# When the weights of pass 3's second half and of pass 4 are fetched, and where B11 is split, in a linear-attention kernel with two MLPs on one Trainium2 core

## The chip, the cores and the metric

One core of a Trainium2 chip runs the whole program. The metric is device microseconds (us) of one execution. TensorE is written PE (PEld for its weight loads), VectorE DVE, ScalarE ACT, GpSimd POOL; SP is the engine whose queue issues nearly all transfers. "Granted clock" is the share of TensorE's full clock that it was given; TensorE has two levels, 2.4 GHz (1.00) and 1.2 GHz (0.50).

## The reference

```python
kv  = einsum('bhsd,bhse->bhde', k, v)          # 8 batches, 8 heads, 576 positions, head 64
out = einsum('bhsd,bhde->bhse', q, kv)
x   = out / sqrt(mean(out*out, -1) + 1e-6) * g_norm      # -> 4608 tokens x 512
h   = x @ w_in1;  x = maximum(0.01*h, h) @ w_out1        # 512 -> 2048 -> 512
h   = maximum(x @ w_in2, 0);  return (h*h) @ w_out2      # 512 -> 2048 -> 512
```

## The kernel before

The 4608 tokens are 9 blocks of 512 (`TB`). Four passes follow each other on TensorE:

- pass 1: attention and the first product (`gemm1`), and on the side the preparation of all weights, which go to DRAM as `w2_d`;
- pass 2 (`second(0, ...)`): the first MLP's second product;
- pass 3 (`first`): the second MLP's first product, then the squared ReLU (`square`), whose result goes to DRAM as `g_d[1]`;
- pass 4 (`second(1, ...)`): the second MLP's second product, to the output.

Every float32 operand is split into a rounded high part (ACT, line 554, suffix h) and a remainder (DVE, line 559, suffix l), and a product is three matmuls: high by high, high by low, low by high. Passes 2 to 4 use a scheme of seven block products for a 2x2 block matrix product (`PRODUCTS`, in the order 6, 1, 2, 7, 5, 4, 3). Its operands are quarters (for tokens of pass 3: B11, B21, B22) and sums of quarters (T1 to T4, made on DVE at line 539). The seven operands of one set of tokens in pass 3 come in the order T2, B11, B21, T3, T1, T4, B22. The results are put together by copies and additions that read the PSUM banks: ACT copies product 1 (`p`, line 605), DVE adds (line 574), and the four finished blocks C11, C22, C21, C12 of `h_C` are squared (ACT 621, 623, 624; DVE 626).

A **slot** is one call of `first` (6 matmuls of 512 columns, or 12 of 256) or `second` (12 matmuls of 256 columns). Each of passes 2 to 4 has 252 slots. Pass 3 begins at slot `t2` and pass 4 at `t3`; at the seam the last calls of `first` alternate with the first calls of `second`. Pass 3 runs over `SETS` (block 0 alone, then pairs of blocks): first all sets with the first half of the weights (14 of 28 tiles), then, from the last set on, with the second half. `again` is true for the one set that stands at that turn. In pass 4, blocks are taken in groups of seven slots; each group's `g_raw` (two loads of 512 KB, `load_g2`, line 512) is read back from DRAM.

The order of all this is written out: every step is an event with a slot number (`at_slot`), the events are sorted, and each engine's instructions stand in that order. An engine, and SP's queue, goes through its own list strictly in order; a waiting instruction holds what stands behind it. What the change touches:

- `fetch` (lines 275 to 281): takes the next tile of weights from the list `wanted` as long as fewer than `w_cap` are held and one of 45 buffers is free (`take_big` hands out the buffer that was returned longest ago), and issues its load of 512 KB (line 280). `cap` and `want` set the bound and the list; `drop_w` returns tiles.
- `tick` (lines 231 to 237), called at each slot: issues the stores that `store` put on a list two slots earlier (line 236). In pass 3 these are the `h_C` blocks, 256 KB each, four for every seven slots. `h_C` has four buffers (`hp`, line 97), so a block can't be written before the store of the one four earlier has landed.
- `prep` (lines 771 to 779): the order in which one set's operands are made: `os` sums, `oh` high parts, `ol` low parts. Lines 815 to 824 give each step its slot, 0.7 slots apart.

```python
at_slot(t0 + 1.5, "cap", 24)                       # 846, at the turn of pass 3
at_slot(t0 + 1.6, "want", (1, 0), NSLOT // 2, NSLOT)
at_slot(t3 - 26, "cap", 20)                        # 849, for pass 4
at_slot(t3 - 25.9, "want", (1, 1), 0, NSLOT)
at_slot(t3 + 6, "cap", 28)
```

Of the kernel before, what the change touches and what calls it, by code (L numbers as in the profile page):

```python
# [18 lines left out]
def tile_linear_attention_two_mlps(  # L19
# [108 lines left out]
    def take_big(shape, dtype, name):  # L128
        n = big_free.pop(0)
        return big.tile(shape, dtype, tag=f"s{n}", name=name), n  # L130

    def give_big(*ns):
        big_free.extend(ns)
# [95 lines left out]
        stores.append([out, in_, slots, 0])  # L229

    def tick():
        for x in stores:
            x[3] += 1
        while stores and stores[0][3] > 1:
            to, src, slots, _ = stores.pop(0)
            nc.sync.dma_start(out=to, in_=src)  # L236
            give_big(*slots)

    def sum_w2(w, n, name):
        a, b, op = SUMS[name]  # L240
        if (w, n) not in w_s:
            w_s[w, n] = take_big([P, 4, 2, P], F32, f"ws_{w[0]}{w[1]}_{n}")
        t = w_s[w, n][0][:, int(name[1]) - 1]
        nc.vector.tensor_tensor(out=t, in0=w_operand(w, n, a), in1=w_operand(w, n, b), op=op)
        w_s[w, n, name] = t
# [15 lines left out]
            give_big(w_s.pop((w, n))[1])  # L261


    wanted = []
    w_cap = [0]

    def want(w, a, b):
        wanted.extend((w, n) for n in range(a, b))
        fetch()

    def cap(n):
        w_cap[0] = n
        fetch()

    def fetch():
        while wanted and w_used[0] < w_cap[0] and big_free:
            w, slot = wanted.pop(0)
            t, n = take_big([P, 2, TB], F32R, f"w2_{w[0]}{w[1]}_{slot}")
            w_used[0] += 1
            nc.sync.dma_start(out=f32(t), in_=w2_d[w][slot])  # L280
            w_t[w, slot] = t, n

    def drop_w(*keys):
        for key in keys:
            give_big(w_t.pop(key)[1])
            w_used[0] -= 1
        fetch()
# [190 lines left out]
    def leaky(j, m):  # L478
        h = hp.tile([P, TB], F32, tag="h", name=f"h{j}_{m}")
        nc.scalar.activation(out=h, in_=h_ps.pop((j, m)), func=AF.Prelu, alpha=0.01)  # L480
        store(
            g_d[0][j][m // 4][:, m % 2, :, (m // 2 % 2) * U:(m // 2 % 2 + 1) * U],
            h.rearrange("p (t u) -> p t u", t=2),
        )
        tick()
# [95 lines left out]

    def first(u, z, pairs, x, free):
        tick()
        pr = ORDER[x]
        bk = "b" if pr in (6, 7, 4) else "a"
# [55 lines left out]
    def second(ph, gg, x, free):  # L641
        j, n = gg
        tick()
        pr = ORDER[x]
        if n == 0:
# [61 lines left out]
    with tc.manual_schedule():  # L707
# [44 lines left out]
        for s, (j, m) in enumerate(slots):  # L752
            if m == 0 and j + 1 < NB:
                at0, pace = (s - 4, 4) if j else (s, 4)
# [13 lines left out]
        def at_slot(t, *st):  # L768
            ev.append((t, st))

        def prep(z):
            n = (("os", 1), ("os", 2), ("oh", 2), ("oh", 11), ("ol", 2), ("oh", 0), ("ol", 11),
                 ("os", 3), ("ol", 0), ("oh", 3), ("oh", 1), ("ol", 3), ("ol", 1), ("os", 4))
            if z == "S":
                n += (("oh", 22), ("oh", 4), ("ol", 22), ("ol", 4))
            else:
                n += (("oh", 4), ("oh", 22), ("ol", 4), ("ol", 22))
            names = {11: "A11", 0: "A12", 22: "A22"} if z == "S" else {11: "B11", 0: "B21", 22: "B22"}
            return [(kind, names.get(x) or f"{z}{x}") for kind, x in n]

        def second_pass(t0, ph, blocks):
            gs = [(j, n) for j in blocks for n in range(NQ)]
            steps = prep("TS"[ph])
            for x, gg in enumerate(gs):
                at0 = t0 + NPR * x
                at_slot(max(at0 - 14, t0 - 12), "gl", ph, gg)
                for n, (kind, name) in enumerate(steps):
                    at_slot(at0 - 8 + n * NPR / len(steps) + 0.3, kind, ph, gg, name)
                at_slot(at0 - 8 + NPR + 0.31, "rawd", ph, gg)
                for n in range(NPR):  # L790
                    at_slot(at0 + n + 0.1, "s2", ph, gg, n, True)
                if gg[0] == blocks[-1]:
                    at_slot(at0 + NPR, "wd", (ph, 1), gg[1])
            return t0 + NPR * len(gs)
# [11 lines left out]
        for x, (half, z) in enumerate(insts):  # L806
            t0 = t2 + NPR * u
            pairs = [(n,) for n in range(half * NPAIR // 2, (half + 1) * NPAIR // 2)]
            if len(SETS[z]) == 1:
                pairs = [pairs[0] + pairs[1], pairs[2] + pairs[3]]  # L810
            again = x + 1 < len(insts) and insts[x + 1][1] == z
            if not (x and insts[x - 1][1] == z):
                lead = 11 if x and len(SETS[insts[x - 1][1]]) == 1 else 15
                at_slot(t0 - lead - XLEAD if x else t0 - 19, "xl", z)
                for y, (kind, name) in enumerate(prep("T")):
                    at0 = t0 - lead + 0.7 * y
                    if kind in ("oh", "ol"):
                        nth = [PRODUCTS[p][1] for p in ORDER].index(name)
                        if nth >= EARLY:
                            at0 = max(at0, t0 - 6.6 + 2 * (nth - EARLY) + (0.8 if kind == "ol" else 0))  # L820
                    elif name == "T4":
                        at0 = t0 - lead + 0.7 * y
                        at0 = max(at0, t0 - 6.6 + 2 * (4 - EARLY) + 0.9)
                    at_slot(at0, kind, 2, z, name)
                    if kind == "ol" and name == "T3":
                        at_slot(at0 + 0.01, "sd", z, "T3")
                    if kind == "ol" and name == "T1":
                        at_slot(at0 + 0.01, "sd", z, "T1")
                    if kind == "ol" and name == "T4":
                        at_slot(at0 + 0.01, "sd", z, "T4")  # L830
                        at_slot(at0 + 0.02, "sd", z, "T2")
                    if kind == "ol" and name == "B22":
                        at_slot(at0 + 0.01, "rawd", 2, z)
            for y, mine in enumerate(pairs):
                free = y == len(pairs) - 1 and not again
                for n in range(NPR):
                    at0 = t2 + NPR * u + 2 * n
                    at_slot(at0, "f", u, z, mine, n, free)
                    c = {2: "C11", 5: "C22", 4: "C21", 3: "C12"}.get(ORDER[n])
                    if c:  # L840
                        at_slot(at0 + 1.2, "sq", u, z, mine, c)
                if again or x == len(insts) - 1:
                    at_slot(t2 + NPR * u + 12.4, "wd3", mine)
                u += 1
            if again:
                at_slot(t0 + 1.5, "cap", 24)
                at_slot(t0 + 1.6, "want", (1, 0), NSLOT // 2, NSLOT)
        t3 = t2 + NPR * u
        at_slot(t3 - 26, "cap", 20)
        at_slot(t3 - 25.9, "want", (1, 1), 0, NSLOT)  # L850
        at_slot(t3 + 6, "cap", 28)
        second_pass(t3, 1, [j for half, z in insts if half for j in SETS[z]])
        ev.sort(key=lambda e: e[0])

# [26 lines left out]
        def drop_pairs(ps):  # L881
# [11 lines left out]
            "scale": scale_w, "join": join_w, "w": split_w, "g1": gemm1, "lk": leaky,  # L893
            "ws": sum_w2, "w2": split_w2, "want": want, "cap": cap, "xl": load_x, "gl": load_g2,
            "rawd": drop_raw, "os": sum_op, "sd": drop_sum, "oh": hi_op, "ol": lo_op,
            "tick": tick, "f": first, "sq": square, "s2": second, "wd": drop_group, "wd3": drop_pairs,
        }
        load = {
            "kv": (load_kv, 0, 2), "scale": (load_w, 0, 1), "a": (load_q, 1, 1)
# [21 lines left out]
        for kind, *args in prog:  # L921
            do[kind](*args)
            if kind in free_by:
                _, n, tiles = load[free_by[kind]]
# [34 lines left out]
```

## Time and profile before

| | us |
|---|---|
| median of 3 runs (lowest, highest) | 1663.08 (1662.37, 1665.74) |
| the profiled execution, its own time | 1666.68 |
| its span, first to last instruction | 1664.9 |
| PE busy in it | 1593.8 (96%) |
| DVE, ACT, POOL busy | 1218.7, 768.1, 255.1 |

In the trace, pass 2 begins at about 562 us, pass 3 at about 928, pass 4 at about 1286. A row of a timeline is: start, length, engine, line, operation, written tile, read tiles, shape, count; in brackets the idle time of that engine before it and what ended it. PE shows a matmul's length with its pipeline, so matmuls overlap; the step from one start to the next is what one costs. A row of windows gives the busy time of each engine in a stretch with the number of instructions, then the granted clock, the mean busy share of the 16 DMA engines, and what they moved in GB/s.

### The profile page before, as it was taken

To read this page: it belongs to the slowest core of one execution; us is meant where nothing else is said; L and a number is where in the kernel's file an instruction comes from. 1 tells how busy PE (TensorE), PEld (TensorE's weight loads), DVE (VectorE), ACT (ScalarE), POOL (GpSimd) and SP (SyncE) were. 2 spreads that over 40 slices of the span, in tenths; PEclk is the share of its full clock that TensorE was granted. 3 is DMA by queue.
4 is the path that set the end of the run, shared out by engine and by line. 5 is a ranking of instruction groups with operands and counts; after the bars stand their busy time and mean duration, and the time that the engine had idled before them with its cause. 6 is when DMAs were issued, how large, how long until landed. Compare 5 with 4: busy or idle time off the path is not lost. (4 is left out here: it accounts for less than half of the span.)

```text
span 1664.9 us, 27914 instructions
## 1 busy us (share of the span) xinstructions
PE 1593.8 (96%) x10504; PEld 1429.5 (86%) x10504; DVE 1218.7 (73%) x1867; ACT 768.1 (46%) x1439; POOL 255.1 (15%) x272
## 2 busy tenths in 40 slices
PE   4999999999999999999999999999999899999999
PEld 2778777777777899999999988778878899999999
DVE  5967777776675388878788877647776688888886
ACT  4555565655654344444434444424444344433433
POOL 3444544544554000000000000000000000000000
PEclk8999999999999999999999999999999999999999
DMA  7677988989977943333346654564449833333342
GB/s 215 197 210 242 329 283 276 318 268 303 349 248 269 410 155 127 127 128 129 135 136 227 211 173 162 193 212 152 158 158 326 312 127 128 131 130 127 133 133 83
DMA packets 249447, 338.45 MB, mean 203 GB/s; under 512 B 55264, under 2 KB 180192, under 8 KB 249312
## 3 DMA queue, kind: packets, MB, share of 16 engines
q1 hardware_dynamic: 249152, 336.67, 60.7%
q8 instruction: 83, 1.36, 0.3%
q14 instruction: 52, 0.43, 0.1%
q10 hardware_dynamic: 160, 0.00, 0.0%
HBM read 198.18 MB, written 138.41 MB: 202 GB/s over the span
## 5 line engine op out<-in xcount | busy, mean ns | idle before, releaser
L468 PE MATMUL hps<-xh,w 128*128 128x512 f32 x1152 | 374.0, 396 | 8.5 <-DVE sqo L413 6.2
L468 PEld LDWEIGHTS hps<-xh,w 128*128 128x128 f32 x1152 | 217.4, 189 | 57.1 <-DVE sqo L413 6.7
L468 PE MATMUL hps<-xl,w 128*128 128x512 f32 x576 | 226.0, 392 | 1.3 <-POOL xl L428 1.3
L468 PEld LDWEIGHTS hps<-xl,w 128*128 128x128 f32 x576 | 109.0, 189 | 23.1 <-POOL xl L428 2.1
L574 DVE TENSOR_TENSOR h_C<-aps,u 128x512 f32<-128x512 f32 x72 | 49.5, 688 | 70.4 <-DMA g<-h_C 37.4
L480 ACT ACTIVATE h<-hps 128x512 f32<-128x512 f32 x144 | 85.0, 592 | 34.0 <-DMA g<-h 30.8
L173 DVE TENSOR_SCALAR w_raw<-w_raw 128x512 uint32<-128x512 uint32 x64 | 48.6, 760 | 33.4 <-ACT wt L172 33.3
L574 DVE TENSOR_TENSOR u<-bps,p 128x512 f32<-128x512 f32 x72 | 49.5, 687 | 25.1 <-PE bps L595 13.7
L413 DVE SCALAR_TENSOR_TENSOR sqo<-ssps,sqo 128x512 f32<-128x512 f32 x36 | 24.9, 691 | 56.8 <-ACT sqo L412 55.9
L393 POOL TENSOR_TENSOR sqs<-sqo,sqs 128x512 fp32r<-128x512 f32 x36 | 49.2, 1367 | 85.5 <-DVE sqs L392 79.7
L190 DVE SCALAR_TENSOR_TENSOR wt<-wt,w_raw 128x512 uint32<-128x512 uint32 x64 | 58.0, 907 | 2.2
L595 PE MATMUL aps<-op_B22h,w 128*128 128x512 f32 (+1 forms) x160 | 53.4, 383 | 4.9 <-DVE h_C L574 4.9
L428 POOL TENSOR_TENSOR xl<-sqo,xh 128x512 fp32r<-128x512 f32 x36 | 48.4, 1344 | 60.8 <-ACT xh L427 43.4
L595 PE MATMUL aps<-op_B21h,w 128*128 128x512 f32 (+1 forms) x160 | 52.2, 375 | 4.9 <-ACT p L605 4.9
L612 ACT ACTIVATE h_C<-aps 128x512 f32<-128x512 f32 x36 | 21.6, 600 | 72.7 <-issue 29.9
L176 DVE SCALAR_TENSOR_TENSOR w_raw<-w_raw 128x512 uint32<-128x512 uint32 x64 | 52.9, 827 | 2.2
L605 ACT ACTIVATE p<-aps 128x512 f32<-128x512 f32 x36 | 21.3, 591 | 71.6 <-PE aps L595 71.6
L595 PE MATMUL bps<-op_T4h,w 128*128 128x512 f32 (+1 forms) x160 | 51.4, 370 | 1.2 <-DVE u L574 1.2
L595 PE MATMUL bps<-op_T3h,w 128*128 128x512 f32 (+1 forms) x160 | 52.0, 374 | 0.0
L595 PE MATMUL bps<-op_T2h,w 128*128 128x512 f32 (+1 forms) x160 | 51.3, 370 | 0.0
L595 PE MATMUL aps<-op_T1h,w 128*128 128x512 f32 (+1 forms) x160 | 51.0, 368 | 0.0
L595 PE MATMUL aps<-op_B11h,w 128*128 128x512 f32 (+1 forms) x160 | 51.0, 368 | 0.0
(1408 smaller groups left out, 4204.1 us busy)
## 6 DMA issues: line engine op xcount, KB each, us to landing
g_raw<-g SPq DMA_DIRECT2D x144, 512.0 KB, 5.6
w<-w SPq DMA_DIRECT2D x84, 512.0 KB, 7.3
g<-h SPq DMA_DIRECT2D x144, 256.0 KB, 5.7
g<-h_C SPq DMA_DIRECT2D x144, 256.0 KB, 2.4
w_raw<-in_moe_w_in_dram SPq DMA_DIRECT2D x32, 512.0 KB, 6.1
w_raw<-in_moe_w_out_dram SPq DMA_DIRECT2D x32, 512.0 KB, 5.9
w<-whS SPq DMA_DIRECT2D x64, 256.0 KB, 5.5
x_raw<-x SPq DMA_DIRECT2D x32, 512.0 KB, 6.1
```

What stands on the lines that cost most here:

```text
L173: nc.vector.tensor_scalar(out=upper, in0=upper, scalar1=0x80000000, scalar2=None, op0=ALU.bitwise_and)
L176: nc.vector.scalar_tensor_tensor(out=lower, in0=lower, scalar=29, in1=upper, op0=ALU.logical_shift_right, op1=ALU.bitwise_or,)
L190: nc.vector.scalar_tensor_tensor(out=t, in0=t, scalar=3, in1=lower, op0=ALU.logical_shift_left, op1=ALU.bitwise_or,)
L393: nc.gpsimd.tensor_tensor(out=sqs[:, 1], in0=sqo[:, 0], in1=f32(sqs[:, 0]), op=ALU.subtract)
L413: nc.vector.scalar_tensor_tensor(out=z, in0=ps, scalar=EPS, in1=z, op0=ALU.add, op1=ALU.mult)
L428: nc.gpsimd.tensor_tensor(out=xl, in0=osb, in1=f32(xh), op=ALU.subtract)
L468: nc.tensor.matmul(out=ps, lhsT=w[:, wh, c * P:(c + 1) * P], rhs=x_t[j][xh, c // 2][0][:, c % 2, :], start=(c == 0 and y == 0), stop=(c == ...
L480: nc.scalar.activation(out=h, in_=h_ps.pop((j, m)), func=AF.Prelu, alpha=0.01)
L574: nc.vector.tensor_tensor(out=t, in0=x, in1=y, op=ALU.add)
L595: nc.tensor.matmul(out=ps[:, p], lhsT=w[:, wh, c, :], rhs=t[xh][:, c, :], start=(fresh and p == 0 and c == 0 and y == 0), stop=(p == len(p ...
L605: nc.scalar.activation(out=p1, in_=ps, func=AF.Copy)
L612: nc.scalar.activation(out=h, in_=ps, func=AF.Relu)
```

## The change

Loads of weights can now be paced. `w_pace` is zero at first (no pacing). From the turn of pass 3 on it is 2: after a fetch, the next one is allowed two slots later; `tick` calls `fetch` at each slot. Just after pass 4's begin it becomes 1. The bounds change with it: 22 in place of 20 at `t3 - 26`, 24 at `t3 - 3`, and 28 at `t3 + 1` in place of `t3 + 6`. And in pass 3 the high part of B11 is made first of all steps of a set (it stood behind the two sums T1 and T2 and T2's high part); the three steps that it passes move back by one place (0.7 slots).

```diff
     def tick():
+        slot_n[0] += 1
...
             give_big(*slots)
+        if w_pace[0]:
+            fetch()
...
+    w_pace = [0]
+    w_next = [0]
+    slot_n = [0]
+
+    def set_pace(n):
+        w_pace[0] = n
...
         while wanted and w_used[0] < w_cap[0] and big_free:
+            if slot_n[0] < w_next[0]:
+                break
+            w_next[0] = slot_n[0] + w_pace[0]
             w, slot = wanted.pop(0)
...
-                for y, (kind, name) in enumerate(prep("T")):
+                todo = prep("T")
+                todo.insert(0, todo.pop(3))
+                for y, (kind, name) in enumerate(todo):
...
             if again:
+                at_slot(t0 + 1.4, "pace", 2)
                 at_slot(t0 + 1.5, "cap", 24)
...
-        at_slot(t3 - 26, "cap", 20)
+        at_slot(t3 - 26, "cap", 22)
         at_slot(t3 - 25.9, "want", (1, 1), 0, NSLOT)
-        at_slot(t3 + 6, "cap", 28)
+        at_slot(t3 - 3, "cap", 24)
+        at_slot(t3 + 1, "cap", 28)
+        at_slot(t3 + 1.1, "pace", 1)
```

No instruction is added or taken away on any engine; PE's and POOL's orders are the same. What moves is shown at three places.

**SP's queue at the turn of pass 3** (w_10_15 is the second of the 14 tiles of the second half; g<-h_C is a store of line 236). Before:

```order
L280 DMA w_10_15_11662<-w_10_15_148 128x1024
L280 DMA w_10_16_11664<-w_10_16_149 128x1024
L280 DMA w_10_17_11666<-w_10_17_150 128x1024
L280 DMA w_10_18_11668<-w_10_18_151 128x1024
L280 DMA w_10_19_11670<-w_10_19_152 128x1024
L280 DMA w_10_20_11672<-w_10_20_153 128x1024
L280 DMA w_10_21_11674<-w_10_21_154 128x1024
L280 DMA w_10_22_11676<-w_10_22_155 128x1024
L236 DMA g_6_1_250<-h_C_11655 128x2x256
L236 DMA g_5_1_246<-h_C_11697 128x2x256
```

After:

```order
L293 DMA w_10_15_11675<-w_10_15_148 128x1024
L237 DMA g_6_1_250<-h_C_11655 128x2x256
L293 DMA w_10_16_11696<-w_10_16_149 128x1024
L237 DMA g_5_1_246<-h_C_11683 128x2x256
L237 DMA g_7_0_253<-h_C_11692 128x2x256
L293 DMA w_10_17_11718<-w_10_17_150 128x1024
L237 DMA g_6_1_250<-h_C_11704 128x2x256
L293 DMA w_10_18_11737<-w_10_18_151 128x1024
```

Nine loads stood together ahead of the first store (w_10_14 with these eight); now two stand ahead of it, and one or two stores follow each load.

**SP's queue ahead of pass 4** (w_11_0 is the first tile of pass 4's weights). Before:

```order
L280 DMA w_11_0_13179<-w_11_0_161 128x1024
L280 DMA w_11_1_13181<-w_11_1_162 128x1024
L280 DMA w_11_2_13183<-w_11_2_163 128x1024
L280 DMA w_11_3_13185<-w_11_3_164 128x1024
L280 DMA w_11_4_13187<-w_11_4_165 128x1024
L280 DMA w_11_5_13189<-w_11_5_166 128x1024
L236 DMA g_4_3_244<-h_C_13163 128x2x256
```

After:

```order
L293 DMA w_11_0_13179<-w_11_0_161 128x1024
L237 DMA g_4_3_244<-h_C_13163 128x2x256
L293 DMA w_11_1_13192<-w_11_1_162 128x1024
L237 DMA g_3_3_240<-h_C_13189 128x2x256
L293 DMA w_11_2_13214<-w_11_2_163 128x1024
L237 DMA g_1_2_231<-h_C_13200 128x2x256
L237 DMA g_4_3_244<-h_C_13210 128x2x256
L293 DMA w_11_3_13234<-w_11_3_164 128x1024
```

Six loads stood ahead of a store; now one does. The same goes on up to w_11_27; the loads of group (7, 3)'s `g_raw` now stand behind 22 of pass 4's tiles, where they stood behind all 28.

**ACT in pass 3, at the set of blocks 3 and 4.** Before:

```order
L621 ACTIVATE h_C_10816<-h_C_10816 128x512
L554 ACTIVATE op_2_T2h<-sT_2_2_10841 128x1024
L554 ACTIVATE op_2_B11h<-x_raw_00_10727 128x1024
L605 ACTIVATE p_4_10875<-aps_1_10868 128x512
L612 ACTIVATE h_C_10898<-aps_1_10868 128x512
```

After:

```order
L634 ACTIVATE h_C_10816<-h_C_10816 128x512
L567 ACTIVATE op_2_B11h<-x_raw_00_10727 128x1024
L567 ACTIVATE op_2_T2h<-sT_2_2_10852 128x1024
L618 ACTIVATE p_4_10875<-aps_1_10868 128x512
L625 ACTIVATE h_C_10898<-aps_1_10868 128x512
```

The copy `p` now stands directly behind T2's high part. On DVE, one squaring (line 626) of the running set now stands ahead of the first sum of the next set, where it stood between its two sums.

## Rows read from the trace of the kernel before

**Rows 1.** Timeline of PE at the turn of pass 3, and later, ahead of pass 4.

```profile
1079.62 0.39 PE L595 MATMUL aps<-op_B21h,w 128*128 128x512 f32 x1
1084.41 0.80 PE L595 MATMUL aps<-op_B22h,w 128*128 128x512 f32 x1 [4.40 <-DVE h_C L574]
...
1264.24 0.50 PE L595 MATMUL aps<-op_B22h,w 128*128 128x512 f32 x1 [0.48 <-DVE h_C L574]
```

**Rows 2.** Windows: the wait at the turn, the stretch behind it, ahead of pass 4, behind its first wait.

```profile
1075.00:1084.40 9.40, 5.01 (x23) 3.81 (x21) 0.73 (x2) 0.60 (x1) 0.00 (x0) 0.95 1.01 384
1084.40:1091.00 6.60, 6.59 (x17) 5.22 (x18) 3.51 (x6) 2.37 (x4) 0.00 (x0) 0.55 0.57 183
...
1270.00:1292.00 22.00, 21.98 (x113) 18.53 (x113) 14.62 (x23) 9.49 (x17) 0.00 (x0) 1.00 1.04 390
...
1299.70:1306.60 6.90, 6.87 (x31) 6.32 (x32) 3.10 (x6) 2.35 (x4) 0.00 (x0) 0.59 0.70 230
```

**Rows 3.** Timeline of SP's queue at the turn of pass 3.

```profile
1067.84 4.91 SPq L280 DMA_DIRECT2D w<-w  x9
1073.75 12.19 SPq L236 DMA_DIRECT2D g<-h_C  x5
```

**Rows 4.** Stores of line 236 issued in 930 to 1065, 1073 to 1080, 1254 to 1262, 1270 to 1292, in turn.

```profile
DMA to landing us min/median/max: 2.1/2.3/7.8
...
DMA to landing us min/median/max: 7.8/8.8/9.8
...
DMA to landing us min/median/max: 6.9/7.1/8.4
...
DMA to landing us min/median/max: 5.7/8.1/8.8
```

**Rows 5.** Timeline of DVE ahead of pass 4, and of PE there.

```profile
1278.57 0.69 DVE L539 TENSOR_TENSOR sS_(7, 0)_13385<-g_raw,g_raw 128x512 f32<-128x512 f32 x1 [0.47 <-DMA g_raw<-g]
...
1285.86 0.69 DVE L574 TENSOR_TENSOR h_C<-bps,p 128x512 f32<-128x512 f32 x1 [0.87 <-DMA g<-h_C]
...
1290.21 0.69 DVE L574 TENSOR_TENSOR h_C<-aps,u 128x512 f32<-128x512 f32 x1 [1.86 <-DMA g<-h_C]
...
1298.95 0.68 DVE L574 TENSOR_TENSOR h_C<-bps,p 128x512 f32<-128x512 f32 x1
...
1299.73 2.90 PE L659 MATMUL ps<-w,op_(7, 0)_S 128*128 128x256 f32 x12 [3.90 <-ACT op_(7, 1)_S L554]
```

**Rows 6.** Timeline of ACT, then of PE, at the second set of pass 3.

```profile
968.77 1.06 ACT L554 ACTIVATE op_T2h<-sT 128x1024 fp32r<-128x1024 f32 x1 [3.96 <-DVE sT L539]
969.73 1.04 ACT L554 ACTIVATE op_B11h<-x_raw 128x1024 fp32r<-128x1024 f32 x1
970.68 0.58 ACT L605 ACTIVATE p<-aps 128x512 f32<-128x512 f32 x1
...
969.96 0.39 PE L595 MATMUL bps<-op_T4l,w 128*128 128x512 f32 x1
970.18 0.39 PE L595 MATMUL bps<-op_T4h,w 128*128 128x512 f32 x1
971.31 0.50 PE L595 MATMUL aps<-op_B21h,w 128*128 128x512 f32 x1 [0.74 <-ACT p L605]
```

**Rows 7.** Waits of PE in 960 to 1060, then in 1180 to 1240: in total, times, longest.

```profile
PE aps L595 <- ACT p L605: 2.2, 3, 0.7
...
PE aps L595 <- ACT p L605: 1.5, 2, 0.7
```

**Rows 8.** Windows around two short waits of PE in pass 1.

```profile
241.00:248.00 7.00, 5.46 (x35) 3.91 (x34) 4.51 (x6) 4.44 (x11) 4.38 (x6) 0.76 1.03 382
...
279.00:283.00 4.00, 1.71 (x11) 1.28 (x10) 3.63 (x7) 3.79 (x11) 2.97 (x4) 1.00 0.80 229
```

**Rows 9.** Line 280 in 1060 to 1330; then a line of the waits of SP's queue.

```profile
DMA to landing us min/median/max: 3.7/7.5/10.5
...
SPq L280 <- PE ps L659: 14.4, 12, 5.4
```

More of the change, by code (lines that the diff above doesn't have):

```diff
@@ L778, in prep @@
             names = {11: "A11", 0: "A12", 22: "A22"} if z == "S" else {11: "B11", 0: "B21", 22: "B22"}
+            assert n[3] == ("oh", 11)
             return [(kind, names.get(x) or f"{z}{x}") for kind, x in n]
@@ L895, in tile_linear_attention_two_mlps @@
             "rawd": drop_raw, "os": sum_op, "sd": drop_sum, "oh": hi_op, "ol": lo_op,
-            "tick": tick, "f": first, "sq": square, "s2": second, "wd": drop_group, "wd3": drop_pairs,
+            "tick": tick, "pace": set_pace, "f": first, "sq": square, "s2": second, "wd": drop_group, "wd3": drop_pairs,
         }
```

## The prediction

> **What bounds the kernel now.** I read the page first: TensorE is busy 96% of the span, so a change pays only where PE stands still or runs at its lower clock. Then the timeline of PE through pass 3 and into pass 4, looking for steps from one matmul start to the next that are longer than the usual 0.22 us [rows 6]; then, for each such place, the timelines of the engine that ended the wait. Three kinds of place turn up where the change works.
>
> *The turn of pass 3.* PE starts a matmul at 1079.62 and the next at 1084.41 [rows 1]: 4.79 us for a step of 0.22, a loss of 4.57. Behind it the granted clock is 0.55 for 6.6 us [rows 2], mostly the lower level, which costs another 0.45 x 6.6 = 2.97. The cause is in SP's queue: nine weight loads go out at 1067.84, and the stores of `h_C` come behind them [rows 3]. Nine loads of 512 KB are 4.72 MB, about 12 us at the 384 GB/s of that stretch [rows 2]. Those stores land after 7.8 to 9.8 us, against a median of 2.3 in the quiet part of pass 3 [rows 4]. There are four `h_C` buffers, so DVE can't write the next block, and PE waits for DVE.
>
> *The seam to pass 4.* PE idles 3.90 us before 1299.73 [rows 5], and the clock is 0.59 for the next 6.9 us, a loss of 0.41 x 6.9 = 2.83 [rows 2]. The row names ACT, but the addition on DVE at 1298.95 ends at 1299.63, 0.1 before PE starts: it empties a PSUM bank that this product takes over. DVE was late because it had itself waited 0.47 for `g_raw` and 0.87 and 1.86 for stores of `h_C` [rows 5], in a stretch in which transfers ran at 390 GB/s without a break [rows 2] and stores took a median of 8.1 us [rows 4].
>
> *The start of each set.* At 971.31 PE starts 1.13 us after the matmul before, 0.91 too late, behind `p` on ACT [rows 6]. ACT made T2's high part (968.77), then B11's (969.73), and only then `p` (970.68). The same wait, 0.7 us of idle, stands three times in 960 to 1060 and twice in 1180 to 1240 [rows 7]: five times 0.9.
>
> **The change, part by part.**
>
> *B11 ahead.* ACT idles 3.96 us before T2's high part, waiting for DVE's sum [rows 6]. B11's high part (1.04 us) needs no sum, only `x_raw`, so it goes into that idle time and costs nothing as long as the idle time is over 1.04 and `x_raw` is there: its loads are issued 10 slots (over 13 us) ahead of the step, while the slowest load of a weight, as large, takes 10.5 [rows 9]. `p` moves from 970.68 to 969.73, directly behind T2, and ends at 970.31; PE wants it at 970.18 + 0.22 = 970.40. So the whole 0.9 goes, five times: **4.5 us**. Bounds: nothing, if PE is then held by something else at once; 4.5 at most. I take 4.5, since rows 6 name no other wait. The squaring that changes places with a sum on DVE is as long a job in the same stretch; the second sum ends when it did. Cost nothing, covered by the same idle time of ACT.
>
> *Pacing at the turn.* The 14 loads are spread over 28 slots. Two slots (12 matmuls of 512 columns at 0.22 to 0.23: 2.7 us) now carry one load of 0.524 MB and on average 8/7 stores of 0.262, together 0.82 MB or 303 GB/s, under the 390 shown [rows 2]. A store then has at most one load ahead, 0.524 / 0.39 = 1.3 us, and lands after 2.3 + 1.3 = 3.6. Where stores took 6.9 to 8.4 us, at 1254 to 1262 [rows 4], PE idled 0.48 at 1264 [rows 1]; so 3.6 holds nobody. The wait and its lower clock go: 4.57 + 2.97 = 7.5. Bounds: 4.6, if the clock falls all the same, and 7.5. I take **7.2**, leaving 0.3 for small leftovers.
>
> *Pacing ahead of pass 4.* For the first 14 of the 26 slots, seven loads and ten stores are 6.3 MB in 19 us, 330 GB/s: no queue builds up. The last twelve slots carry six weights, six loads of `g_raw` and six stores, 7.86 MB in about 16.5 us, 476 GB/s, over the 390 shown. At 390 this takes 20.2 us, so 3.7 us of backlog are left at the end, and a store there lands after up to 2.3 + 3.7 = 6.0. That is under the 6.9 to 8.4 that cost 0.48. DVE's three waits go, 0.47 + 0.87 + 1.86 = 3.20, and the addition that PE waits for comes 3.2 earlier; PE keeps 0.7 of idle time there, since DVE's own work is then the limit. Does the clock still fall? In pass 1, one idle time of about 1.5 us (7.00 less 5.46 busy) goes with a fall to the lower level, another of 2.3 (4.00 less 1.71) doesn't [rows 8]. So I take a coin's toss over a fall half as long as the one here (1.4 us), 0.7. The gain is 3.2 + 2.83 - 0.7 = **5.3**. Bounds: 0, if DVE is held as before, and 3.9 + 2.83 = 6.7.
>
> A rule of the Trainium skill speaks against this term. Its page "DMA: Bandwidth & Descriptors", section "Where 436 GB/s comes from", has the HBM side bind transfers between HBM and SBUF at about 358 GB/s per core. By that figure the twelve slots would leave 5.5 us of backlog, a store would land after 7.8, and part of DVE's waits would stay. The trace shows 390 over 22 us, so the measurement decides here.
>
> *Are the weights in time?* The tile with the least room is fetched 12 slots before its use (w_11_17, 18, 24 and 25), over 16 us; loads of line 280 land within 10.5 us at the worst [rows 9], with the queue full. Cost nothing; without that room, PE would wait for the difference. Reads of `g_raw` move ahead of some weights and come earlier, which pays nothing on PE.
>
> Sum: 4.5 + 7.2 + 5.3 = 17.0. The profiled execution took 1666.68, so 1649.7 by its own time; it lies 3.6 above the median of the runs, 1663.08. Against that median I forecast **1646.1**. If the plain runs lose less in these very waits, the gain is smaller; the range allows for that.
>
> **The rivals.**
>
> *The tail stays full.* Ahead of pass 4 the same bytes move in the same time; if stores still take 8 us there, the seam is not mended and 5.3 is lost: 1651.4. For it: 476 GB/s wanted against 390 [rows 2]. Against: the six and four loads in a bunch ahead of a store are gone. The skill's rule above would end here. Chance 0.20.
>
> *B11 buys nothing,* because `p` is then late for another reason or PE is caught one product later: 1646.1 + 4.5 = 1650.6. Against it: rows 6 fit to 0.1 us. Chance 0.08.
>
> *No pacing in effect.* The change orders the queue; it doesn't tie SP to PE. If the stores wait for nothing, SP runs through loads and stores at once and the bunch comes back: only B11 counts, 1663.1 - 4.5 = 1658.6. Against: each store waits for a block that is computed slot by slot. Chance 0.04.
>
> *A fetch holds the stores: slower.* SP is in order, and each paced load now stands directly ahead of a store. If its buffer is still in use, SP waits and the store isn't issued. Such a hold of 5.4 us exists before, on PE at line 280 [rows 9]. A store that lands after more than about 7 us starts to cost, so a hold over 7 - 3.6 = 3.4 us decides; one of 5 us or more costs what the turn costs now, 7.5. The gain of 17.0 is eaten by the third, and three give 1646.1 + 22.5 = 1668.6. Against it: buffers are handed out longest-returned first, with several free. Chance 0.03.
>
> **How the numbers follow.** The forecast has 0.62; the rest, 0.03, is a gain eaten by some new wait, within 0.2% (3.3 us, about what a measurement of this kernel can tell from no change). Faster by over 0.2%: 0.62 + 0.20 + 0.08 + 0.04 = 0.94. Same: 0.03. Slower: 0.03. The upper bounds of the terms, 4.5 + 7.5 + 6.7 = 18.7, with 2 us for the spread of the runs and small waits of the same kind (the 0.48 at 1264), give 1642; below that lies little. Upwards the range takes in the first two rivals with 1.5 us on top: 1653. No pacing and slower stay outside.
>
> **What would show it.** PE's step at the starts of sets falls from 1.13 to about 0.23. At the turn of pass 3 PE has no idle time over 1 us, the clock stays 1.00, and stores land in a median under 4 us. Ahead of pass 4 DVE's waits on `h_C` stores go, and PE idles about 0.7 before the fifth product of group (7, 0). The prediction is wrong if stores still land after 8 us at either place, if PE waits on weights, or if a new gap follows a mended one.

## The result, and the profile after

The changed kernel takes 1648.55 us (median of 5 runs, 1646.02 to 1649.03), the kernel before 1663.08 (median of 5, 1662.28 to 1666.38). The ratio is 0.9903, 95% interval 0.9890 to 0.9917: 16.1 us, between 13.8 and 18.3. The forecast was 1646.1, inside 1642 to 1653. The profiled execution of the changed kernel took 1646.02 us, of before 1666.68.

The waits of PE from the start of pass 3 to the first groups of pass 4 (915 to 1310 us) tell most of it. A row of waits is: who waited, for whom, us in total, times, the longest. Before:

```profile
PE aps L595 <- DVE h_C L574: 4.9, 2, 4.4
PE aps L595 <- ACT p L605: 4.9, 8, 0.7
PE ps L659 <- ACT op_(7, 1)_S L554: 3.9, 1, 3.9
PE bps L595 <- DVE u L574: 1.2, 3, 0.4
```

After (a line number from 280 on is 13 higher than before, so 574 is now 587; 236 is 237):

```profile
PE ps L672 <- ACT op_(7, 1)_S L567: 1.7, 1, 1.7
PE aps L608 <- ACT p L618: 1.5, 4, 0.7
PE bps L608 <- DVE u L587: 0.6, 2, 0.3
PE aps L608 <- DVE h_C L587: 0.4, 1, 0.4
```

14.9 us of waiting became 4.2. The wait at the turn is gone, and so are the five waits on `p` of [rows 7] (a shorter one, at 1267, is new); 1.7 us of the 3.9 ahead of pass 4 are left.

**The start of a set.** Timelines of ACT and of PE at the second set, where [rows 6] showed a step of 1.13 us:

```profile
961.79 1.05 ACT L567 ACTIVATE op_B11h<-x_raw 128x1024 fp32r<-128x1024 f32 x1
965.70 1.06 ACT L567 ACTIVATE op_T2h<-sT 128x1024 fp32r<-128x1024 f32 x1 [2.86 <-DVE sT L552]
966.66 0.58 ACT L618 ACTIVATE p<-aps 128x512 f32<-128x512 f32 x1
```

```profile
966.99 0.39 PE L608 MATMUL bps<-op_T4h,w 128*128 128x512 f32 x1
967.29 0.50 PE L608 MATMUL aps<-op_B21h,w 128*128 128x512 f32 x1
```

B11's high part now lies in ACT's idle time, `p` follows T2 directly, and PE's step is 967.29 - 966.99 = 0.30.

**The turn of pass 3.** Timelines of PE between the same two products as in [rows 1], and of SP; windows; stores issued in 1064 to 1095:

```profile
1073.81 0.39 PE L608 MATMUL aps<-op_B21h,w 128*128 128x512 f32 x1
1074.04 0.39 PE L608 MATMUL aps<-op_B22h,w 128*128 128x512 f32 x1
```

```profile
1067.60 0.89 SPq L237 DMA_DIRECT2D g<-h_C  x2
1068.58 0.45 SPq L293 DMA_DIRECT2D w<-w  x1
1069.13 0.62 SPq L237 DMA_DIRECT2D g<-h_C  x1
```

```profile
1065.00:1075.00 10.00, 10.00 (x46) 8.29 (x45) 5.71 (x9) 3.46 (x7) 0.00 (x0) 1.00 0.94 326
1075.00:1085.00 10.00, 10.00 (x46) 8.29 (x45) 4.57 (x7) 3.32 (x7) 0.00 (x0) 1.00 0.98 338
```

```profile
DMA to landing us min/median/max: 2.5/3.9/5.8
```

The step that took 4.79 us takes 0.23, the clock stays at 1.00, and the queue moves 326 to 338 GB/s where it had stood at 384 [rows 2]. Stores land after a median of 3.9 us, against 8.8 [rows 4].

**Ahead of pass 4.** Timelines of DVE and PE; windows ahead of the wait and behind it; stores issued in 1250 to 1262, then in 1262 to 1284:

```profile
1263.37 0.69 DVE L552 TENSOR_TENSOR sS_(7, 0)_13379<-g_raw,g_raw 128x512 f32<-128x512 f32 x1 [0.70 <-DMA g_raw<-g]
...
1280.83 0.68 DVE L587 TENSOR_TENSOR h_C<-bps,p 128x512 f32<-128x512 f32 x1
```

```profile
1281.61 1.67 PE L672 MATMUL ps<-w,op_(7, 0)_S 128*128 128x256 f32 x12 [1.70 <-ACT op_(7, 1)_S L567]
```

```profile
1262.00:1282.00 20.00, 18.05 (x103) 15.47 (x102) 17.84 (x30) 9.95 (x18) 0.00 (x0) 1.00 1.04 388
1281.60:1288.50 6.90, 6.89 (x52) 6.64 (x53) 5.47 (x9) 2.41 (x4) 0.00 (x0) 1.00 1.03 414
```

```profile
DMA to landing us min/median/max: 3.5/5.2/6.3
...
DMA to landing us min/median/max: 4.5/6.6/9.1
```

DVE waits for no store there any more; its wait for `g_raw` is still there, 0.70. Its addition ends at 1280.83 + 0.68 = 1281.51, and PE starts 0.10 later, as in [rows 5] (the operation of ACT that PE's row names had ended at 1280.89). PE's idle time is 1.70 in place of 3.90, and the clock behind it is 1.00 in place of 0.59 [rows 2]. Pass 4 begins at 1271.24 in this profile: of the stores issued in 1262 to 1284, the longest ahead of that took 7.1, and the one of 9.1 was issued behind it, at 1282.92.

### The profile page after: what moved, and what is told of

It is laid out like the page before. It is cut to its first block, busy times and chain, and to the rows that moved or that the text cites. A ratio compares the mean times of both kernels' runs of the same rounds, so it can differ in the third digit from the quotient of the medians.

```text
span 1644.2 us, 27915 instructions
## 1 busy us (share of the span) xinstructions
PE 1586.1 (96%) x10504; PEld 1424.0 (87%) x10504; DVE 1219.0 (74%) x1867; ACT 768.1 (47%) x1439; POOL 254.9 (16%) x272
## 3 DMA queue, kind: packets, MB, share of 16 engines
q8 instruction: 83, 1.36, 0.3%
## 5 line engine op out<-in xcount | busy, mean ns | idle before, releaser
L481 PEld LDWEIGHTS hps<-xl,w 128*128 128x128 f32 x576 | 109.2, 190 | 23.1 <-POOL xl L441 1.9
```

Source lines behind the costliest of these rows:

```text
L481: nc.tensor.matmul(out=ps, lhsT=w[:, wh, c * P:(c + 1) * P], rhs=x_t[j][xh, c // 2][0][:, c % 2, :], start=(c == 0 and y == 0), stop=(c == ...
```

## The experiments

Each kernel below was timed beside the kernel before. Us off is (1 - ratio) times before's median in the same runs. That median was 1663.1 to 1664.2 in the four groups of runs, so two rows are best compared by their us off, each of which is known to about 2 us.

| kernel | median us | ratio (95% interval) | us off |
|---|---|---|---|
| the change | 1648.55 | 0.9903 (0.9890 to 0.9917) | 16.1 |
| B11 alone | 1658.40 | 0.9969 (0.9957 to 0.9980) | 5.2 |
| pacing at the turn alone | 1657.10 | 0.9961 (0.9948 to 0.9973) | 6.5 |
| pacing ahead of pass 4 alone | 1659.26 | 0.9973 (0.9963 to 0.9984) | 4.5 |
| six `h_C` buffers alone | 1643.81 | 0.9888 (0.9872 to 0.9903) | 18.6 |
| control: one large tile fewer | 1662.09 | 0.9989 (0.9980 to 0.9999) | 1.8 |
| B11, six buffers, no pacing | 1640.94 | 0.9860 (0.9845 to 0.9876) | 23.3 |
| the change, six buffers | 1641.30 | 0.9861 (0.9848 to 0.9874) | 23.1 |
| the change, one fetch a slot at the turn | 1646.55 | 0.9897 (0.9883 to 0.9910) | 17.1 |
| the change, six buffers, groups 4 slots earlier | 1638.87 | 0.9850 (0.9835 to 0.9864) | 25.0 |
| five buffers alone | 1645.86 | 0.9893 (0.9877 to 0.9910) | 17.8 |
| the change, eight buffers, groups 4 slots earlier | 1641.53 | 0.9868 (0.9853 to 0.9883) | 22.0 |

The kernels with six and five buffers have 44 large tiles in place of 45, the one with eight has 43.

**One part at a time.** The theory is the sum of the prediction: three separate losses, each with its own cure.

*B11 alone*: of the change only this, with the old bounds and no `pace`.

```diff
-                for y, (kind, name) in enumerate(prep("T")):
+                todo = prep("T")
+                todo.insert(0, todo.pop(3))
+                for y, (kind, name) in enumerate(todo):
```

> Only B11's split is moved ahead of the sums; the weights are fetched in bunches as before. My theory: the wait of PE on ACT's p at a set's start (0.9 us, five times) goes, and nothing else: about 4.5 us off the time before, PE's idle 4.4 us at the turn of pass 3 and 2.3 us ahead of the fifth product of group (7,0) stay within 0.5 us. Rival, B11 buys nothing (the work behind the sums is only shifted): under 1 us off, and the waits come back one or two products later with the same sum. Second rival, B11 hides part of the pacing's gain: more than 6 us off.

5.2 us came off. Waits of PE in 915 to 1310:

```profile
PE aps L608 <- DVE h_C L587: 5.0, 2, 4.4
PE ps L672 <- ACT op_(7, 1)_S L567: 3.9, 1, 3.9
PE aps L608 <- ACT p L618: 1.2, 3, 0.7
```

The waits on `p` fell from 4.9 us to 1.2; the two other waits, which pacing is to cure, are untouched. Neither rival fits. (The 2.3 us that this expectation and the third name ahead of pass 4 is 3.90 in [rows 5].)

*Pacing at the turn alone*, without B11:

```diff
+                at_slot(t0 + 1.4, "pace", 2)
                 at_slot(t0 + 1.5, "cap", 24)
...
+        at_slot(t3 - 26.1, "pace", 0)
         at_slot(t3 - 26, "cap", 20)
```

> Only the first bunch, the one at the turn of pass 3, is paced at one fetch for every two slots; the bunch ahead of pass 4 and B11 are as before. My theory: the stores behind the fetches land in under 4 us, PE's idle time of 4.4 us at the turn falls under 1 us and the stretch of lower clock after it goes with it: 7.2 us off the time before, 4.6 us if the lower clock comes elsewhere instead. Rival, the stores were late for a reason that pacing does not touch: PE idles 4 us or more at the turn as before, and the time is within 1 us of before's.

6.5 us came off. The same view:

```profile
PE aps L608 <- ACT p L618: 4.9, 8, 0.7
PE ps L672 <- ACT op_(7, 1)_S L567: 3.9, 1, 3.9
PE aps L608 <- DVE h_C L587: 1.4, 1, 1.4
```

No wait is left at the turn. The 1.4 stands at 1256, ahead of pass 4, where the bunch is still whole.

*Pacing ahead of pass 4 alone*, without the event at the turn and without B11:

```diff
-        at_slot(t3 - 26, "cap", 20)
+        at_slot(t3 - 26.1, "pace", 2)
+        at_slot(t3 - 26, "cap", 22)
...
-        at_slot(t3 + 6, "cap", 28)
+        at_slot(t3 - 3, "cap", 24)
+        at_slot(t3 + 1, "cap", 28)
+        at_slot(t3 + 1.1, "pace", 1)
```

> Only the bunch ahead of pass 4 is paced; the bunch at the turn and B11 are as before. My theory, with the row of the changed kernel now known (PE idles 1.70 us behind VectorE's C21 at that place): the three waits of VectorE on stores go (0.47, 0.87 and 1.86 us), PE's idle of 2.3 us there falls to about 1.7 us, and what comes off the time is the lower clock after it, 2.8 us, and 1 to 2 us of idle: 4 us in a profile with that clock at full, 1 to 2 us in one where it falls all the same. Rival, the wait at that place is VectorE's own work and no store's: under 1 us off, VectorE without waits on stores and PE's idle there as before.

4.5 us came off. The same view:

```profile
PE aps L608 <- DVE h_C L587: 4.7, 1, 4.7
PE ps L672 <- ACT op_(7, 1)_S L567: 1.7, 1, 1.7
```

The wait at the turn is there as before; the one ahead of pass 4 is cut to 1.7, and the clock in the 6.8 us behind it is 1.00. DVE's two waits on stores there are gone, but 0.44 of the 0.47 is left: that one was for `g_raw`, not for a store. The bounds move in the same edit; what they do without the pacing was not tried. The parts add up: 5.2 + 6.5 + 4.5 = 16.2, and all three together gave 16.1.

**Is it the buffers?** The prediction's chain has a link that pacing alone doesn't test: late stores cost time because they hold `h_C` buffers.

```diff
-    NBIG = 45
+    NBIG = 44
...
-    hp = ctx.enter_context(tc.tile_pool(name="hp", bufs=4))
+    hp = ctx.enter_context(tc.tile_pool(name="hp", bufs=6))
```

> Order, bunches and all work as before, but six buffers in place of four for the sums h_C that wait for their stores, and one of the 45 large tiles fewer to make room. My theory: what PE waits for at the turn is a buffer of h_C held by a store that stands behind fetched weights. Then two more buffers (about 3 slots of VectorE's work each) let VectorE go on while the stores land in 7 to 8 us as before; PE's idle at the turn falls from 4.4 us to under 1 us with no fetch moved, and 5 to 9 us come off. Rival, PE or VectorE is held there by the fetches themselves, not through the buffers: the wait stays at 3 us or more, and the time within 2 us of before's. If stores land as late as before and the wait is gone, the theory stands.

18.6 us came off, more than twice the upper end. PE's waits in 915 to 1310, then the stores issued in 1055 to 1100 and who waited for them:

```profile
PE aps L608 <- ACT p L618: 4.8, 8, 0.7
PE ps L672 <- ACT op_(7, 1)_S L567: 1.5, 1, 1.5
```

```profile
  DVE h_C L587: 9.2, 2
...
DMA to landing us min/median/max: 2.1/6.6/10.7
```

Stores land as late as before (up to 10.7), DVE still waits for them (9.2 us in two waits), and PE doesn't idle at the turn. So the link holds. The wait ahead of pass 4 went to 1.5 as well. The rest of the gain lies ahead of pass 3, where the change does nothing. `hp` also holds pass 1's blocks `h` between ACT's leaky ReLU and their stores. ACT's waits on these stores in 20 to 600, in the changed kernel, then with six buffers alone:

```profile
ACT h L493 <- DMA g<-h: 27.5, 16, 4.1
```

```profile
ACT h L493 <- DMA g<-h: 2.6, 1, 2.6
```

And PE's first wait of pass 3, in the same two profiles:

```profile
928.28 0.38 PE L608 MATMUL aps<-op_B21h,w 128*128 128x256 f32 x1 [0.75 <-ACT p L618]
```

```profile
922.55 0.38 PE L608 MATMUL aps<-op_B21h,w 128*128 128x256 f32 x1 [0.69 <-ACT p L618]
```

In the seven profiles with four buffers this row stands between 928.28 and 932.98, in the five with five or six buffers between 922.55 and 923.72. How a late store reaches PE in pass 1 shows at 172, in the profile of before: ACT waits for the store of an `h`, and behind it in ACT's list stand operations that DVE's work hangs on, and `qhl`, an operand that ACT and then DVE make for PE.

```profile
171.91 0.60 ACT L480 ACTIVATE h<-hps 128x512 f32<-128x512 f32 x1 [1.32 <-DMA g<-h]
...
177.10 0.36 PE L384 MATMUL ops<-qhl,kv 128*128 128x192 f32 x1 [1.22 <-DVE qhl L370]
```

With six buffers PE has no wait at this place. Its waits for `qhl` ahead of pass 3, before, then with six buffers alone:

```profile
PE ops L384 <- DVE qhl L370: 8.1, 8, 2.3
```

```profile
PE ops L397 <- DVE qhl L383: 4.0, 6, 1.1
```

That is 4.1 us. The clock is the other part: before has three falls between 60 and 915 us (0.83 in 240 to 250, 0.79 in 422 to 430, 0.83 in 562 to 572, each a loss of 1.7), the profile with six buffers none. Together this is 9.2, and PE's first wait of pass 3 comes 931.47 - 922.55 = 8.9 earlier than before. That the buffers keep the clock from falling was not tested by itself.

*The control*, with four buffers:

```diff
-    NBIG = 45
+    NBIG = 44
```

> The kernel before with 44 large tiles in place of 45 and four buffers of h_C as before: the control for the run with six buffers, which also gave up one large tile. My theory: the large tile does nothing and the buffers did all, so the time stays within 2 us of before's. Rival: one large tile fewer alone makes fetches start later, and so spreads them: 4 us or more off, with PE's idle at the turn under 3 us.

1.8 us off, and PE idle 3.35 us at the turn. The tile has at most a small part in it.

*Six buffers and B11 without pacing, then with it.* The two lines above (44 tiles, six buffers), once in the kernel with B11 alone, once in the changed kernel:

```diff
-    hp = ctx.enter_context(tc.tile_pool(name="hp", bufs=4))
+    hp = ctx.enter_context(tc.tile_pool(name="hp", bufs=6))
```

> B11 ahead of the sums and six buffers of h_C with 44 large tiles; the weights in bunches as before. My theory: pacing pays only through the buffers that late stores hold, so with six buffers nothing of it is left to gain: the run with six buffers alone less five waits of 0.9 us, 1643.8 - 4.5 = 1639.3 us, and the changed kernel with six buffers within 2 us of it. Rival: pacing does something beside (weights in time, TensorE's clock): this kernel is 3 us or more slower than the changed kernel with six buffers.

> The changed kernel as it is, with six buffers of h_C and 44 large tiles. My theory: its waits on stores in pass 3 are gone already, so six buffers take from it only what they took in the stretch before pass 3, where the run with six buffers came to pass 3 at 921.6 us and the changed kernel's profile at 927.3: about 5.7 us off the changed kernel, 1643 us, if that stretch was the buffers' doing, and 0 if it was chance. Rival: buffers and pacing add up in pass 3 also: 1636 us or less.

1640.94 and 1641.30: the same. On top of the buffers B11's move pays 23.3 - 18.6 = 4.7, as expected (from PE's first wait of pass 3 to the end, the two profiles differ by 719.3 - 715.3 = 4.0). Pacing pays nothing on top of them: what it cures, the buffers had cured. Against the changed kernel the six buffers take 23.1 - 16.1 = 7.0, near the 5.7 that pass 1 had let expect and far from 12.

*Five buffers.*

```diff
-    NBIG = 45
+    NBIG = 44
...
-    hp = ctx.enter_context(tc.tile_pool(name="hp", bufs=4))
+    hp = ctx.enter_context(tc.tile_pool(name="hp", bufs=5))
```

> The kernel before with five buffers of h_C in place of four (44 large tiles), order and bunches as before: the dose between the control (1662.1 us) and the run with six (1643.8 us). My theory: a buffer more is one h_C more that VectorE can form ahead of the late stores. PE's idle at the turn was 3.3 to 4.4 us with four and nothing with six; with five it falls to between 0.5 and 2.5 us without the lower clock behind it, and the time lies between 1646 and 1656 us. Rival: the stores leave in such groups that one buffer more is of no use until there are two: idle over 3 us, time over 1657 us.

1645.86, 0.14 below the range. PE's only wait at the turn, and the stores there:

```profile
1079.63 0.50 PE L595 MATMUL bps<-op_T4h,w 128*128 128x512 f32 x1 [0.97 <-DVE u L574]
```

```profile
DMA to landing us min/median/max: 2.1/2.7/10.7
```

One buffer more takes the idle time to 0.97, and pass 3 begins as early as with six (the row at 923.33). I had sized the time for pass 3 alone and left pass 1 out.

**How much pacing is needed?** Against the changed kernel:

```diff
-                at_slot(t0 + 1.4, "pace", 2)
+                at_slot(t0 + 1.4, "pace", 1)
...
+        at_slot(t3 - 26.1, "pace", 2)
         at_slot(t3 - 26, "cap", 22)
```

> The changed kernel with one fetch for every slot in place of one for every two, at the turn of pass 3 only. My theory goes by the rate: 524 KB a slot and the stores beside them ask for more than the 390 GB/s that the trace showed over 22 us, so the queue grows through the bunch, the last stores land in 5 to 7 us, and part of the turn's wait comes back: PE idle 1 to 4 us there, 1 to 6 us above the changed kernel. Rival, any order that lets a store stand between fetches is enough: stores land under 4 us, no idle at the turn, within 1 us of the changed kernel.

The rival's time, but not its reason: 17.1 us off against 16.1, no idle time at the turn, yet the queue is full and stores land late. Windows in 1070 to 1090, stores issued in 1076 to 1084, and DVE's first wait on a store with the addition ahead of it:

```profile
1070.00:1090.00 20.00, 20.00 (x90) 16.55 (x89) 8.32 (x13) 5.26 (x10) 0.00 (x0) 1.00 1.04 406
```

```profile
DMA to landing us min/median/max: 7.3/7.6/8.9
```

```profile
1076.18 0.68 DVE L587 TENSOR_TENSOR h_C<-bps,p 128x512 f32<-128x512 f32 x1
1080.10 0.69 DVE L587 TENSOR_TENSOR h_C<-aps,u 128x512 f32<-128x512 f32 x1 [3.23 <-DMA g<-h_C]
```

The backlog came, and was larger than worked out from the rate (5 to 7 us), but PE didn't pay. Two things decide that: how long DVE waits, and which addition it waits with. The wait of before at the turn (its PE row is in [rows 1], 4.40 idle) holds C22, and so does the one that is left with pacing at the turn alone, shown with its PE row:

```profile
1083.67 0.69 DVE L574 TENSOR_TENSOR h_C<-aps,u 128x512 f32<-128x512 f32 x1 [9.13 <-DMA g<-h_C]
```

```profile
1255.53 0.69 DVE L587 TENSOR_TENSOR h_C<-aps,u 128x512 f32<-128x512 f32 x1 [6.08 <-DMA g<-h_C]
...
1256.28 0.50 PE L608 MATMUL aps<-op_B22h,w 128*128 128x512 f32 x1 [1.36 <-DVE h_C L587]
```

9.13 - 4.40 = 4.73 and 6.08 - 1.36 = 4.72. In the seven profiles with four buffers PE idled behind C22 ten times in pass 3, from 4.75 us (where DVE waited 9.47) down to 0.23 (4.95), and the difference is 4.72 or 4.73 each time. A wait of 4.69 with C22, at 1223.52 in the profile of before, left PE no idle time. So at this addition PE has 4.7 us in hand, and above that each us costs a us.

The 3.23 with one fetch a slot stands at another addition: C12, directly behind C21's. With six buffers DVE's two waits stand there too; in the run with B11 they are 5.03 and this one:

```profile
1074.48 0.69 DVE L587 TENSOR_TENSOR h_C<-aps,u 128x512 f32<-128x512 f32 x1 [5.07 <-DMA g<-h_C]
```

None of them cost PE anything. By the kernel, PE's next product on the same bank has to wait for C22, while C12 is the last to read its bank. How long a wait at C12 may be was not measured beyond 5.07.

**What is left ahead of pass 4.** The change with six buffers, and for the first two groups of pass 4:

```diff
+                early = 4 if ph and x < 2 else 0
-                at_slot(max(at0 - 14, t0 - 12), "gl", ph, gg)
+                at_slot(max(at0 - 14, t0 - 12) - early, "gl", ph, gg)
```

with `early` subtracted from the slots of their operands too.

> The changed kernel with six buffers of h_C, and the operands of the first two groups of pass 4, (7,0) and (7,1), loaded and prepared four slots earlier; nothing else moved. It tests the reading of the idle time of 1.70 us that is left ahead of pass 4: VectorE works there without a break, C21's addition ends at 1281.51 us and PE starts at 1281.61, so it is VectorE's own queue that holds PE. My theory: with four slots more for the same work the idle falls under 0.5 us, and 1 to 2 us come off the changed kernel with six buffers (1641.3 us). Rival: the groups' data come too late from the stores, the earlier work waits for its loads at the head of VectorE's queue, and the idle stays or grows: within 1 us of 1641.3 or slower.

25.0 us off, 1.9 more than without. PE at the place:

```profile
1274.96 1.70 PE L672 MATMUL ps<-w,op_(7, 0)_S 128*128 128x256 f32 x12 [0.41 <-DVE h_C L587]
```

1.70 became 0.41: it was DVE's own work. This is the fastest kernel here, 25.0 - 16.1 = 8.9 us beyond the change.

*Eight buffers on top of that.*

```diff
-    NBIG = 44
+    NBIG = 43
...
-    hp = ctx.enter_context(tc.tile_pool(name="hp", bufs=6))
+    hp = ctx.enter_context(tc.tile_pool(name="hp", bufs=8))
```

> As the run with the two groups prepared earlier, with eight buffers of h_C and 43 large tiles. My theory: in pass 3 nothing waits on a store any more with six, so nothing comes off there; in the first stage ScalarE still waits 7.9 us in three waits on stores of h, and 0 to 2 us come off. Rival: large tiles are the scarcer thing, weights start later and PE waits for one: slower by 2 us or more.

1641.53, 2.7 slower than with six. The time is the rival's, but PE waits for no weight: ACT's waits on stores of `h` are gone, pass 3 is untouched, and 3.4 us are lost ahead of it (its first wait stands at 926.69 against 923.26). Half of that is a fall of the clock which the profile with six buffers doesn't have: 0.88 in 393 to 407, a loss of 1.7. What takes the rest stays open.

## Why the prediction was right, and where it was off

**B11 ahead, 4.5.** Right. All five waits went, PE's step at the set shown is 0.30 where 0.23 was named, and the part alone gave 5.2 (3.3 to 7.2 by its interval).

**Pacing at the turn, 7.2.** Right in mechanism, and the part alone gave 6.5 (4.5 to 8.7). No idle time, clock 1.00, stores at 3.9 for the 3.6 worked out. The link through the buffers is shown, since two more of them do the same with stores as late as before. Two of its steps were wrong. The price "where stores took 6.9 to 8.4 us, PE idled 0.48" counts the wrong thing: not the landing decides, but which addition DVE waits with, and at C22 what its wait has beyond 4.7 us. With one fetch a slot, stores of 7.3 to 8.9 us cost nothing, so the pacing by two slots is more than needed. And the lower clock's 2.97 is the dearer of two cases. In the run with B11 alone the clock behind the same wait is 0.75, a loss of 0.25 x 6.8 = 1.7, and in the control it is 0.75 too:

```profile
1080.60:1087.40 6.80, 6.37 (x21) 5.09 (x22) 4.15 (x7) 2.38 (x4) 0.00 (x0) 0.75 0.60 207
```

With 1.7 in place of 2.97 the sum would have been 6.3, nearer to the 6.5.

**Pacing ahead of pass 4, 5.3.** The mechanism held, stores that DVE waits for and PE behind it. The sum came near, 4.5 for the part alone (2.7 to 6.2), in part by luck, since two errors nearly cancel. "PE keeps 0.7 of idle time": it kept 1.70, so 2.2 of idle went, not 3.2. The step that was off is "the addition comes 3.2 earlier". The wait for `g_raw`, 0.47 of the 3.20, didn't go at all. And waits on one engine don't add up to what the next engine gains: in the four profiles with the bunch and four buffers there (before, B11 alone, pacing at the turn alone, the control) DVE's two waits on stores come to 2.2 to 2.8 us, and PE idled 3.86 to 3.90 in all four. What is left is DVE's own work, as the run with the groups prepared earlier shows. The other error is the coin toss over the clock: its 0.7 was not needed. The clock fell behind all eight waits of 3.3 us or more at these two places in the 13 profiles, and behind none of the ten there of 1.0 to 1.7. The 2.83 for the lower clock, too, is the dearer case: with B11 alone and in the control the clock there is 0.75, a loss of 1.7.

The count of bytes had a slip that changes nothing: four stores for every seven slots are eight in the first 14, not ten, which makes 304 GB/s in place of 330. In the last twelve slots stores were to land within 6.0. Ahead of pass 4's begin the longest took 7.1; behind it, where one fetch a slot is allowed, 9.1. I read this as the bunching that is left, which is argued; DVE waited for none of them.

This bears on the rule weighed there, of the Trainium skill's page "DMA: Bandwidth & Descriptors", section "Where 436 GB/s comes from": with its 358 GB/s the prediction had estimated 7.8. This case moved 388 GB/s over 20 us there, 414 behind, and 406 in 20 us with one fetch a slot; the figure doesn't bind here.

**Weights in time.** Right: PE waits on no load of a weight in 915 to 1310.

**The sum.** From PE's first wait of pass 3 to the end, the two profiles differ by 20.7 - (931.47 - 928.28) = 17.5 us, for 17.0 forecast. The other 3.2 lie in passes 1 and 2, which the change leaves alone: the profile of before has two falls of the clock more there, about 3.4 us. The medians differ by 14.5 and the ratio gives 16.1, with 17.5 inside its interval. So the 1646.1 came out 2.45 below the change's median, and whether plain runs lose less in these waits than the profiled execution, as the prediction allowed, is not shown; those runs have no trace.

**The rivals.** None came. "The tail stays full" had its condition in part (a median of 6.6, up to 9.1) and not its price. The hold of SP by a fetch stayed short: its longest wait at a fetch in 1055 to 1330 is 1.3 us, where 3.4 was to decide.

What the prediction didn't see is the larger gain beside it. It named the four buffers as the link and then priced only the queue. A fifth buffer, with one large tile given up for it, was worth 17.8 us, as much as the whole change.

## What to carry to other kernels

When an engine waits for a buffer that a late transfer holds, price both cures: spreading the transfers, and one more buffer, which can also help wherever else that pool is used; here one pair of buffers made the pacing worthless. Measure the slack from rows: at one addition here, the waiter's wait less the idle time of the engine behind it was 4.7 us each time, and lateness below that was free. Do it for each operation that can be held, since at the next addition a longer wait cost nothing. Where several waits on one engine go, don't add them up; ask what work of its own is queued next.

## What the runs showed that was not expected

The clock's falls in passes 1 and 2 come and go between executions of the same instructions: before had three between 60 and 915 us, the change one, with these passes unchanged. In the profiles with five or six buffers there was none. Behind one and the same wait at the turn, the clock over the next 6.8 us was 0.56 and 0.58 in two profiles, and 0.75 in two others.
